# Attention and a gated projection on one core: nine full projection blocks per two batches, a second staging tile for V, and a re-dealt order

## The chip, the cores and the metric

The kernel runs on one core of a Trainium2 chip. Five instruction queues matter: PE (TensorE, matmuls and transposes), DVE (VectorE), ACT (ScalarE), POOL (GpSimd) and SP (SyncE), which here issues every DMA. Each queue is in order; they meet only at semaphores. The metric is the device time of one execution in microseconds, as a median over several runs.

## The reference

What is computed, with batch 8, 8 heads, 576 positions, head size 64 and model width 512:

```python
scores = scale * np.matmul(q, k.transpose(0, 1, 3, 2))
cum = np.cumsum(np.maximum(s, 0.0), axis=-1)
bias = -(cum[:, :, :, None] - cum[:, :, None, :])
scores = np.where(causal, -1e9, scores + np.minimum(bias, 0.0))
attn = softmax(scores)
x = (attn @ v), heads side by side            # (8, 576, 512)
gate = sigmoid(causal 5-tap convolution of x along the sequence, per channel)
out = (gate * (x @ w_val)) @ w_out
```

## The kernel before

Work is cut into 32 units n = 4b + p: batch b (8 of them) and pair of heads p (4 per batch). For each unit:

- q and k are cast to bf16 (L518; eight small casts for batch 0, two large ones for each later batch), transposed on PE (L557, unit by unit; the last 64 rows of q and k, the "tail", for a whole batch at once in L546) and copied from PSUM to the tile QKT (L561 and L549).
- Scores are computed key by key into pairs of PSUM banks (L566), in three steps of 1024 columns (512 for each of two heads), and each step goes through one exp on ACT (L592), 96 in all. The last 64 x 64 corner of every pair goes through a smaller exp (L578). POOL zeroes the future on the diagonal blocks (the mask, L598; L603 for the corners).
- The decay from s is folded into V: POOL or DVE multiplies the staging tile vst (f32) by w into Vp (bf16) with a column of ones (L528). The attention product (L613) is 30 matmuls per unit. DVE takes the reciprocal of the sums (L618) and normalizes into xn (L623).
- x is transposed (L631) and copied to xT (L635). Four taps of the convolution follow, each one DVE instruction (L647, L649) or two POOL ones (L644, L645); then a tanh on ACT (L653).
- Per batch: the value projection in eight groups of four matmuls (val, L660), each followed by glu on DVE (L666), which multiplies by the gate. Then the output projection.

The output projection before (L669 to L680) works batch by batch. 576 positions are five blocks; the fifth has 64 positions of its own. It is computed as a full block of 128 columns beginning at 448, and only its upper 64 rows are copied to an ot tile and stored: 40 blocks in all, each of four matmuls of 512 columns, a copy on ACT or DVE (L677) and a store (L680). Three ot tiles take turns.

One staging tile vst holds V of one batch; the loads for batch b wait for the four products of batch b - 1 that read it (L716).

What sets the order is a planner in the kernel (class Plan). Every task carries an engine, an assumed duration, a due time, the tasks it depends on and what it takes (PSUM banks, work tiles). The planner walks through time: each engine that is free takes the ready task with the smallest due time, and the resulting order is written out as the program. Due times are the unit's number plus an offset from the table DUE (with extra terms for the first two and the last two batches); where a task may run on several engines, a string of digits in CHOICE names the engine for each instance. On the chip, engines follow that order and wait for semaphores only; the planner's durations play no part there.

Places to look at: the head (L687 to L700: batch 0's loads in small pieces), the later batches' loads and casts (L702 to L720), the loops over units (L733 to L773), val and glu (L775 to L784), the projection (L785 to L792), and a check of all reciprocals near the end (L799 to L812), whose result the program reads before it finishes.

Of the kernel before, what the change touches and what calls it, by code (L numbers as in the profile page):

```python
# [10 lines left out]
FP32 = mybir.dt.float32  # L11
BF16 = mybir.dt.bfloat16
# [6 lines left out]
B, H, S, D = 8, 8, 576, 64  # L19
DM = 512  # L20
# [185 lines left out]
def pcol(kb, qb):  # L206
    if kb == qb:
        return kb * 128
    if qb == 4:
# [16 lines left out]
DUE = dict(w=-69.33, lwv=-4.26, lwo=-2.61, cwv=56.85, cwo=86.75, av=-11.07, norm=-74.98, xt=-16.64,  # L226
           xe=-86.49, tap=14.23, dtap=-1.47, tanh=-72.16, val=7.76, dval=0.88, out=11.28, dout=0.61,
           oute=87.55, qt=-4.79, qe=133.25, tt=-0.4, te=-149.08, s4=-20.03, vp=-7.1, cast=76.15, lqk=-1.56,
           mask=-123.76, lv=-49.38, av_e=7.71, av_l=6.68, cast_e=-31.51, cast_l=0.54, dout_e=-1.01,
           dout_l=-28.82, dtap_e=-7.57, dtap_l=16.17, dval_e=0.26, dval_l=0.84, lqk_e=-7.13, lqk_l=48.32,  # L230
           lv_e=98.37, lv_l=-92.01, mask_e=11.67, mask_l=11.41, norm_e=50.24, norm_l=38.99, out_e=0.39,
           out_l=42.92, oute_e=70.67, oute_l=-23.24, qe_e=-66.52, qe_l=-3.56, qt_e=4.39, qt_l=0.95,
           s4_e=8.96, s4_l=-14.16, tanh_e=58.9, tanh_l=56.45, tap_e=3.56, tap_l=-27.97, te_e=47.36,
           te_l=62.72, tt_e=19.75, tt_l=0.79, val_e=-3.44, val_l=-1.96, vp_e=-68.8, vp_l=29.32, xe_e=13.94,
           xe_l=0.22, xt_e=-5.82, xt_l=-13.61)


def due_of(b, name):
# [5 lines left out]
STAY = (0.1, 54.75)  # L244

CHOICE = dict(vp0="0100",
              cast="12200210",
              wts="00",
              te="10001100",
              qe="10100010000000001000100000100010",  # L250
              xe="00100010001000010000000000010010",
              tap="00000000100000000000001000000000000000010000100000000000000010000000000000001000001000001000100000000010000010010010001101110000",
              oute="1000001110101000010100010100011010000010")


class Plan:
# [22 lines left out]
    def run(self):  # L279
# [33 lines left out]
        while len(self.order) < len(self.tasks):  # L313
            started, later = False, []
            for e in engs:
# [36 lines left out]
                if e == "SP":  # L352
                    idle_at[e] = now + 0.06
                    dma_free = max(dma_free, now + 1.2) + us
                    t["done"] = dma_free + 0.8
                else:
                    idle_at[e] = t["done"] = now + us
# [21 lines left out]
def main_path(ctx, tc, q, k, v, s, moe_w_val, moe_conv_w, moe_w_out, out, okcnt):  # L379
# [9 lines left out]
    plan = Plan(dict(P=3, gp=2, th=6, ot=3, qkf=3))  # L389
# [484 lines left out]
```

## Time and profile before

| | us |
|---|---|
| median of 6 runs | 209.55 (209.17 to 211.56) |
| the profiled execution | 209.78 |
| its span | 208.1 |
| first exp of 1024 columns starts | 8.99 |
| last exp ends | 178.7 |
| last attention product ends | 180.7 |
| last copy of an output block ends | 202.4 |

A page's group line reads: source line, engine, operation, written tile <- read tiles, shape, count | total busy us, mean ns of one | idle time of the engine just before, and what ended most of it. Busy times of neighbours can overlap, so the busy time of an engine is less than the sum of its rows. In a view of busy time by stage, each row gives the stage, its length, busy us and number of instructions for each engine, then the granted TensorE clock, the share of time that the 16 DMA engines were busy, and their rate. In a timeline a row is start, length, engine, line, operation, and in brackets how long the engine was idle before and who released it.

The TensorE clock was granted in full for nearly all of the span (0.986 on average). DMA engines were busy without a pause up to about 110 us, since loads run ahead as far as buffers allow, and little used after that. Loads of V are made of runs of 256 bytes; 47,109 of 69,230 packets are under 512 bytes.

### The profile page before, as it was taken

How to read it: one execution, taken by the hardware profiler on the slowest of the kernel's cores; microseconds unless marked ns; L12 is line 12 of the kernel's file. 1: busy time of each engine (PE TensorE's matmuls, PEld its weight loads, DVE VectorE, ACT ScalarE, POOL GpSimd, SP SyncE). 2: the span in 40 equal slices, each digit the busy share in tenths (PEclk: the TensorE clock that was granted, in tenths of full speed). 3: DMA queues.
4: the chain of work that ended last, by engine and by line, in shares of the span. 5: the costliest groups of instructions: out<-in, count | busy, mean ns of one | idle time of the engine just before them, and what ended most of it. 6: DMA issues, size and time to landing. Idle time of an engine off the chain costs nothing.

```text
span 208.1 us, 6007 instructions
## 1 busy us (share of the span) xinstructions
PE 172.4 (83%) x2392; PEld 117.6 (57%) x2411; DVE 177.3 (85%) x311; ACT 163.3 (78%) x205; POOL 161.3 (78%) x179
## 2 busy tenths in 40 slices
PE   1688765899969997789899799989899999979950
PEld 0446553485737765467675657565576555755620
DVE  3847969989889998579999999999999998999710
ACT  3379897788999999987996997899987998553430
POOL 4265595599959998999499999958975898999300
PEclk9999998899999999999999999999999999999997
DMA  4999999999999898999999911941159120222551
GB/s 136 251 268 305 363 158 227 356 253 247 227 284 306 214 288 228 318 336 207 270 373 248 200 58 28 200 132 54 50 126 226 60 79 0 104 101 79 177 185 58
DMA packets 69230, 40.48 MB, mean 195 GB/s; under 512 B 47109, under 2 KB 63493, under 8 KB 69194
## 3 DMA queue, kind: packets, MB, share of 16 engines
q1 hardware_dynamic: 69194, 40.01, 72.1%
q8 instruction: 21, 0.34, 0.7%
q14 instruction: 15, 0.12, 0.2%
HBM read 30.57 MB, written 9.44 MB: 192 GB/s over the span
## 4 chain that ended last, share of the span: by engine, by line
DVE 25%; PE 21%; ACT 21%; issue 8%; DMA 8%; SPq 7%; POOL 7%; ACTq 0%; DVEq 0%
ACT P L592 12%; DVE gp L647 10%; PE banks L660 7%; DMA qkf<-in_moe_w_val_dram 6%; PE banks L672 6%; PE banks L613 4%; ACT QKT L561 3%; DVE xn L623 3%; DVE glu L666 3%; SPq L515 3%; DVE gp L649 3%; ACT th L653 3%; POOL Vp L528 2%; SPq L534 2%; PE banks L566 2%
## 5 line engine op out<-in xcount | busy, mean ns | idle before, releaser
L592 ACT ACTIVATE P<-banks 128x1024 bf16<-128x1024 f32 x96 | 94.9, 1038 | 11.4 <-PE banks L566 9.5
L647 DVE SCALAR_TENSOR_TENSOR gp<-banks,ratio,gp 128x574 f32<-128x574 bf16 (+2 forms) x85 | 67.5, 804 | 2.7 <-POOL gp L645 1.9
L598 POOL TENSOR_SCALAR_AFFINE_SELECT P<-P 128x512 bf16<-128x512 bf16 x64 | 39.4, 638 | 11.7 <-ACT P L592 11.5
L566 PE MATMUL banks<-QKT 64*128 64x128 bf16 (+4 forms) x576 | 38.4, 248 | 9.0 <-ACT P L592 5.3
L660 PE MATMUL banks<-xT,wv 128*128 128x288 bf16 x256 | 41.2, 291 | 2.2 <-DVE glu L666 0.9
L672 PE MATMUL banks<-wo,glu 128*128 128x512 bf16 x141 | 38.2, 379 | 2.6 <-ACT QKT L561 0.8
L528 POOL TENSOR_TENSOR Vp<-vst,w 128x650 bf16<-128x650 f32 x29 | 37.6, 1315 | 1.5 <-DMA vst<-in_v_dram 1.5
L613 PE MATMUL banks<-Vp,P 128*128 128x65 bf16 x960 | 35.7, 195 | 1.3 <-ACT P L592 1.2
L613 PEld LDWEIGHTS <-P 128*128 128x128 bf16 x960 | 33.8, 99 | 5.0 <-issue 2.1
L566 PEld LDWEIGHTS <-QKT 64*128 64x128 bf16 x576 | 20.0, 97 | 26.7 <-issue 20.4
L653 ACT ACTIVATE th<-gp,halfw 128x576 f32<-128x576 f32 x32 | 25.2, 792 | 7.1 <-DVE gp L647 3.6
L660 PEld LDWEIGHTS <-wv 128*128 128x128 bf16 x256 | 22.7, 98 | 13.6 <-issue 5.9
L666 DVE SCALAR_TENSOR_TENSOR glu<-th,banks 128x288 bf16<-128x288 f32 x64 | 27.8, 443 | 0.5 <-PE banks L660 0.3
L561 ACT COPY QKT<-banks 128x1024 bf16<-128x1024 bf16 x25 | 25.4, 1045 | 2.2 <-PE banks L557 2.1
L623 DVE TENSOR_TENSOR xn<-banks,recs 128x640 bf16<-128x640 f32 x32 | 26.2, 818 | 0.3
L677 ACT COPY ot<-banks 128x512 f32<-128x512 f32 (+1 forms) x26 | 15.2, 587 | 11.1 <-PE banks L672 6.9
L672 PEld LDWEIGHTS <-glu 128*128 128x128 bf16 x160 | 14.6, 97 | 15.5 <-issue 2.7
L649 DVE SCALAR_TENSOR_TENSOR gp<-xT,ratio,banks 128x576 f32<-128x576 bf16 x25 | 20.1, 808 | 1.6 <-ACT xT L635 0.9
L644 POOL TENSOR_TENSOR tmp<-xT,ratio 128x576 f32<-128x576 bf16 (+3 forms) x18 | 20.6, 1142 | 0.6 <-DVE xT L635 0.2
L645 POOL TENSOR_TENSOR gp<-tmp,gp 128x573 f32<-128x573 f32 (+2 forms) x11 | 15.7, 1429 | 3.1 <-DVE gp L647 2.3
L631 PE MATMUL banks<-ident,xn 128*128 128x128 bf16 x160 | 14.1, 219 | 3.0 <-DVE xn L623 1.1
L557 PE MATMUL banks<-ident,qb 128*128 128x128 bf16 x128 | 13.1, 227 | 2.1 <-ACT qb L518 1.3
(63 smaller groups left out, 168.0 us busy)
## 6 DMA issues: line engine op xcount, KB each, us to landing
out_dram<-ot SPq DMA_DIRECT2D x32, 256.0 KB, 2.8
qkf<-in_q_dram SPq DMA_DIRECT2D x7, 1024.0 KB, 8.8
qkf<-in_k_dram SPq DMA_DIRECT2D x7, 1024.0 KB, 8.4
vst<-in_v_dram SPq DMA_DIRECT2D x28, 256.0 KB, 5.1
vst<-in_v_dram SPq DMA_DIRECT2D x15, 128.0 KB, 4.2
first<-in_q_dram SPq DMA_DIRECT2D x4, 256.0 KB, 3.3
first<-in_k_dram SPq DMA_DIRECT2D x4, 256.0 KB, 3.5
tail<-in_q_dram SPq DMA_DIRECT2D x8, 128.0 KB, 8.1
```

The lines of the kernel that those rows point to most:

```text
L528: eng.tensor_tensor(Vps[b % 2][:, :, h], vst[:, :, h], w[:, :, b * 8 + 2 * p:b * 8 + 2 * p + 2].unsqueeze(3).to_broadcast([128, NKB, 2, 65 ...
L561: copy[e](QKTs[b % 2][:, :, p, 0:512].rearrange("d w (x j) -> d w x j", j=4), slot["qt", b, p].rearrange("d w (j x) -> d w x j", j=4))
L566: nc.tensor.matmul(ps[:, hh, c0:c0 + nq], QKTs[b % 2][r, 1, p, k0:k0 + 128], QKTs[b % 2][r, 0, p, q0:q0 + nq], **kw)
L592: nc.scalar.activation(out=slot["Pt", n][:, :, step * 512:(step + 1) * 512], in_=slot["s", n, step], func=AF.Exp, scale=0.125)
L598: nc.gpsimd.affine_select(out=d, in_=d, pattern=[[0, 4], [1, 128]], compare_op=ALU.is_ge, fill=0.0, base=0, channel_multiplier=-1)
L613: nc.tensor.matmul(ps[:, hh, qb * 65:qb * 65 + 65], lhsT, Vps[b % 2][:, kb, 2 * p + hh, :], start=(kb == 0), stop=(kb == qb))
L623: nc.vector.tensor_tensor(xns[b % 2][:, :, p * 128:(p + 1) * 128].rearrange("t g (h d) -> t h g d", h=2), pv[:, :, :, 0:64], recs[:, n].un ...
L647: nc.vector.scalar_tensor_tensor(gp[:, o:S], slot["x", n][:, 0:S - o], r, gp[:, o:S], ALU.mult, ALU.add)
L653: nc.scalar.activation(out=th, in_=slot["g", n], func=AF.Tanh, scale=halfw[:, n % 4, :])
L660: nc.tensor.matmul(ps, wv[:, dc, c * 128:(c + 1) * 128], xTs[b % 2][:, dc, 2 + o:290 + o], start=(dc == 0), stop=(dc == 3))
L666: nc.vector.scalar_tensor_tensor(glus[b % 2][:, c, o], slot["t", n][:, o], 1.0, slot["v", n, hf], ALU.add, ALU.mult)
L672: nc.tensor.matmul(ps, glus[b % 2][:, c, WIN[i]:WIN[i] + 128], wo[:, c, :], start=(c == 0), stop=(c == 3))
```

## The change

- **Projection.** Two batches share one glu tile of 1152 positions, so two batches are nine full blocks. An even batch issues four; the odd batch issues five, the first of which spans the boundary. There are 36 blocks instead of 40, all of 128 rows, all stored whole. glu waits for those old blocks only that read the half it overwrites.
- **Last batch.** Each block's projection is four tasks, one per chunk of 128 channels, each due on its own.
- **V.** Two staging tiles. Batch 1's V is loaded pair by pair, in 12 DMAs instead of 5, into the second tile; later batches wait for the products of two batches before. The second tile also serves as the landing place of five of batch 0's small q and k loads, so that its frame (ones and zeros) is set after their casts.
- **ot** has five tiles instead of three.
- **Engines.** Batch 0's tail cast and batch 1's two casts may run on DVE, ACT or POOL.
- **Planner.** A limit on how far SP may run ahead of the transfers (BEHIND), slightly different assumed durations, and new tables DUE, STAY and CHOICE.

The tables set the order and the engines anew. Counted over the built program: first casts DVE 3 to 1, ACT 2 to 5, POOL 3 to 2; tail copies (te) ACT 5 to 8, DVE 3 to 0; QKT copies (qe) 25 on ACT and 7 on DVE in both; xT copies DVE 26 to 18, ACT 6 to 14; taps DVE 110 to 108, POOL 18 to 20; ot copies ACT 26 to 29, DVE 14 to 7. Both of batch 1's casts are given to POOL ("22").

```diff
-STAY = (0.1, 54.75)
-
-CHOICE = dict(vp0="0100",
-              cast="12200210",
+STAY = (1.42, 130.04)
+
+BEHIND = 9.7
+
+CHOICE = dict(cast1="22",
+              tailc="2",
+              vp0="0100",
+              cast="11121201",
...
                 if e == "SP":
-                    idle_at[e] = now + 0.06
                     dma_free = max(dma_free, now + 1.2) + us
+                    idle_at[e] = max(now + 0.06, dma_free - BEHIND)
...
-    plan = Plan(dict(P=3, gp=2, th=6, ot=3, qkf=3))
+    plan = Plan(dict(P=3, gp=2, th=6, ot=5, qkf=3))
...
+    vraw = [one.tile([128, NKB * 8 * 65], FP32, name=f"vst{j}") for j in range(2)]
+    vsts = [a.rearrange("p (i h d) -> p i h d", i=NKB, h=8) for a in vraw]
+
+    def v_frame(j):
+        nc.gpsimd.memset(vsts[j][:, :, :, 64:65], 1.0)
+        nc.gpsimd.memset(vsts[j][0:64, 4, :, :], 0.0)
...
-    glus = two("glu", [128, 4, S], BF16)
+    glu2 = one.tile([128, 4, 2 * S], BF16, name="glu")
+    glus = [glu2[:, :, 0:S], glu2[:, :, S:]]
+    outf = out.rearrange("b s d -> (b s) d")
...
-    def outp(b, i):
-        ps = slot["o", b, i] = bank(("o", b, i), 128, DM)
-        for c in range(4):
-            nc.tensor.matmul(ps, glus[b % 2][:, c, WIN[i]:WIN[i] + 128], wo[:, c, :], start=(c == 0), stop=(c == 3))
+    def outp(b, i, cs):
+        if cs[0] == 0:
+            slot["o", b, i] = bank(("o", b, i), 128, DM)
+        o = (4 * (b % 2) + i) * 128
+        for c in cs:
+            nc.tensor.matmul(slot["o", b, i], glu2[:, c, o:o + 128], wo[:, c, :], start=(c == 0), stop=(c == 3))
...
     def store(b, i):
-        nc.sync.dma_start(out=out[b, kbo[i]:kbo[i] + kbs[i], :], in_=slot["ot", b, i][128 - kbs[i]:128, :])
+        r = b // 2 * 2 * S + (4 * (b % 2) + i) * 128
+        nc.sync.dma_start(out=outf[r:r + 128, :], in_=slot["ot", b, i])
...
+            if b == 1:
+                t = add("POOL", 0.7, DUE["vf"], lambda: v_frame(1), [T["cast", 0, i % 2, i // 2] for i in range(5)])
+                ts = [[add("SP", 1.45, DUE["lv1"] + DUE["lv1d"] * p, lambda p=p: load_v_pair(1, p), [t])] for p in range(4)]
+            else:
+                ts = [[add("SP", 1.45, n0 + due("lv") + i * 0.01, lambda b=b, i=i: load_v_block(b, i),
+                           [T["vp", b - 2, p] for p in range(4)]) for i in range(NKB)]] * 4
...
-        for i in range(NKB):
-            hfs = [(0,), (0,), (0, 1), (1,), (1,)][i]
-            t = T["out", b, i] = add("PE", 0.88, n0 + due("out") + due("dout") * i, lambda b=b, i=i: outp(b, i),
-                                     [T["glu", n0 + c, hf] for c in range(4) for hf in hfs] + [t_wo],
-                                     take=[("bank", ("o", b, i))])
+        for i in range(4 + b % 2):
+            own = [(0,), (0,), (0, 1), (1,), (1,)][i]
+            need = lambda c: [T["glu", n0 + c, hf] for hf in own] + ([T["glu", n0 - 4 + c, 1]] if b % 2 and i == 0 else [])
+            if b == B - 1:
+                t = None
+                for c in range(4):
+                    t = add("PE", 0.22, n0 + DUE["ol"] + DUE["old"] * i + DUE["doc"] * c, lambda b=b, i=i, c=c: outp(b, i, (c,)),
+                            need(c) + [t_wo, t or T["xt", n0 + 3], T["val", n0 + 2, 1]], take=[] if c else [("bank", ("o", b, i))])
+                T["out", b, i] = t
+            else:
+                t = T["out", b, i] = add("PE", 0.88, n0 + due("out") + due("dout") * i, lambda b=b, i=i: outp(b, i, range(4)),
+                                         [d for c in range(4) for d in need(c)] + [t_wo], take=[("bank", ("o", b, i))])
```

## The prediction

> **What bounds the kernel now.** I read the page's busy times first, then the busy time of each engine by stage, then the rows by form, then the instructions of the last 30 us in order.
>
> ```profile
> PE 172.4 (83%) x2392; PEld 117.6 (57%) x2411; DVE 177.3 (85%) x311; ACT 163.3 (78%) x205; POOL 161.3 (78%) x179
> ```
>
> Four engines lie within 16 us of each other, so no single one explains 208.1 us. The stages say more. I cut where batch 0's last exp ends (27.2), where the masks of pair 7, batch 1's last, end (50.5), at 101, and where the last exp (178.7) and the last copy (202.4) end.
>
> ```profile
> core 0: us, PE busy (x) PEld busy (x) DVE busy (x) ACT busy (x) POOL busy (x), PEclk, DMA share, GB/s
> 0.00:27.20 27.20, 16.65 (x226) 11.84 (x226) 18.62 (x34) 17.68 (x24) 14.58 (x31) 1.00 0.94 261
> 27.20:50.50 23.30, 19.39 (x282) 13.60 (x283) 20.83 (x36) 18.56 (x23) 18.78 (x21) 0.93 1.02 244
> 50.50:101.00 50.50, 44.15 (x687) 31.68 (x691) 43.95 (x75) 47.50 (x59) 47.05 (x48) 1.00 1.03 269
> 101.00:178.70 77.70, 71.67 (x1052) 48.45 (x1060) 75.47 (x136) 70.06 (x87) 65.92 (x70) 1.00 0.52 134
> 178.70:202.40 23.70, 20.58 (x155) 12.03 (x154) 18.41 (x34) 9.47 (x16) 14.95 (x12) 1.00 0.40 140
> ```
>
> The reader is to see that DVE is 97% busy (75.47 of 77.70) from 101 us on: it bounds the second half. In the middle, from 27.2 to 178.7 (151.5 us), DVE is busy for 140.3, ACT 136.1, PE 135.2, POOL 131.7. The end is another regime: exps are done, and the deferred projections drain through DVE and PE.
>
> ```profile
> 175.90 2.83 ACT L592 ACTIVATE P<-banks 128x1024 bf16<-128x1024 f32 x3
> ...
> 196.05 4.48 PE L672 MATMUL banks<-wo,glu 128*128 128x512 bf16 x19
> ...
> 199.81 0.58 ACT L677 COPY ot<-banks 128x512 f32<-128x512 f32 x1 [1.25 <-DMA out_dram<-ot]
> 201.82 0.58 ACT L677 COPY ot<-banks 128x512 f32<-128x512 f32 x1 [1.43 <-DMA out_dram<-ot]
> ```
>
> Five blocks of the last projection run in one row, and two copies wait for a store to free one of three ot tiles.
>
> **The change part by part.** Rows that price it:
>
> ```profile
> L672 PE MATMUL banks<-wo,glu 128*128 128x512 bf16 x141 | 38.2, 379 | 2.6 <-ACT QKT L561 0.8 <-DVE gp L647 0.3 <-issue 0.2
> L635 DVE COPY xT<-banks 128x576 bf16<-128x576 bf16 x26 | 11.6, 450 | 2.4 <-PE banks L631 2.3
> L635 ACT COPY xT<-banks 128x576 bf16<-128x576 bf16 x6 | 4.0, 661 | 0.2 <-DVE ok L802 0.2
> L677 ACT COPY ot<-banks 128x512 f32<-128x512 f32 x20 | 11.8, 589 | 9.7 <-PE banks L672 6.6 <-DMA out_dram<-ot 2.7 <-ACT P L592 0.3
> L677 DVE COPY ot<-banks 128x512 f32<-128x512 f32 x12 | 8.2, 684 | 2.2 <-PE banks L672 2.1
> ```
>
> *Projection blocks, 40 to 36.* 16 matmuls and 4 copies go. A lone matmul's 379 ns is latency; in a row they cost 4.48/19 = 0.236 us, so PE loses 16 x 0.24 = 3.8. A 64-row copy costs what a full one does (580 against 589 ns on ACT), so the four copies go at full price. Three of the four blocks leave the stretch after the last attention product: 13 blocks stand there before, 10 after.
>
> *The new choices of engine.* They outweigh the blocks. Copies of ot: ACT 26 to 29, DVE 14 to 7. Copies of xT: ACT 6 to 14, DVE 26 to 18. Tail transposes (te): ACT 5 to 8, DVE 3 to 0. First casts: ACT 2 to 5, DVE 3 to 1, POOL 3 to 2; the first tail cast goes from DVE to POOL. Taps: POOL 18 to 20, DVE 110 to 108. ACT: 3 x 0.589 + 8 x 0.661 + 3 x 0.595 + 3 x 0.618 = +10.7. DVE: 7 x 0.684 + 8 x 0.45 + 3 x 0.417 + 2 x 0.80 + 2 x 0.55 + 0.41 = -12.8. All rows of ACT add to 176.5 against 163.3 busy, those of DVE to 195 against 177.3, because neighbours overlap; scaled so, ACT +9.9 and DVE -11.6. POOL: 2 taps of 1.14 + 1.42, 0.7 for the second frame of V, 0.6 tail cast, less a 0.6 cast: +5.8.
>
> *A rule against the row.* The Trainium skill (Perfetto Trace Analysis, Identifying the Most-Contended Engine) takes the engine of highest occupancy as the one to relieve first. Occupancy names DVE, so by the rule its 11.6 us are worth up to 11.6: 198. The stage rows refuse that: ACT stands 4.2 us behind DVE in the middle and receives nearly all that DVE gives up. I follow the rows.
>
> *The middle, summed.* By the order of instructions of the changed kernel, 3.3 of ACT's 9.9 come before batch 0's last exp, and behind the last exp nothing is added (one ot copy fewer, one xT copy more): 136.1 + 6.6 = 142.7. DVE sheds 4.0 in batch 0 and 0.3 at the end: 140.3 - 7.3 = 133.0. On POOL 16 taps stand ahead of the last mask instead of 12, so 146.3 to 157.0 there; about 1.4 of it is in batch 0: middle 131.7 + 9.3 = 141.0. PE stays near 135. ACT is the new bound, POOL close behind. How dense can a bound engine be? The busiest engine of each middle stage has 20.83 + 47.50 + 75.47 = 143.8 of 151.5, 94.9%; the last stage alone 97.1%. At 97.1% the middle takes 147.0 (-4.5), at DVE's own 92.6% 154.1 (+2.6). I take 95.7%: the first stage's 89.4% I move halfway to full, since V of batch 1, now requested at 26.3 behind the last read of V of batch 0, gets its own tile. 142.7/0.957 = 149.1: **-2.4**.
>
> *Two tiles of V, and the queues.* POOL waits 1.5 us in all for V's loads, so the tile is worth 0 to 2 us, counted in that density. Below zero: V of batch 1 becomes 12 issues in place of 5; SP sends them past the tails of batch 2, w_out and q, k of batch 2, with DMA at 1.02 in that stage. Seven more issues at 0.5 us are 3.5 us of SP time, hidden while those loads are already waiting for engines; w_out is needed at 46.8. If that cover fails, up to 3.5 us of delay reach batch 2's casts on POOL. On POOL four Vp products (4 x 1.3 = 5.2) now stand ahead of batch 1's first mask; ACT runs on into three P tiles meanwhile.
>
> *Head.* SP now sends conv_w and both tails (0.55 + 0.7 + 0.7) before q, and s later. q was cast 2.8 us after issue (2.01 to 4.82), so ACT's first cast moves from 4.82 to about 5.6; tail copy 0.6, cast of k 0.6, transposes 0.8, copy of QKT 1.0 (it was on DVE), a cast and the small exp follow on ACT: first exp at 10.4 against 8.99. Then ACT has fewer gaps (about 7 us in batch 0 against 9.5): 21.0 + 7.0 = 28.0, **+0.8**.
>
> *End.* DVE is 14.96 of 15.2 busy from the last attention product (180.7) to the last five blocks (195.9). The new order has 14.1 us of rows there against 16.2, so -2.1 if DVE stays the limit and 0 if the chain tap, tanh, glu does; PE (2.9 less) and POOL (5.1 less) give room. I take -1.0. With five ot tiles the last copy follows its matmul (200.5) by 0.2 + 0.6 instead of ending at 202.4: -1.1. Together **-2.1**, ends -1.1 and -3.2. The last store's 5.7 us remain.
>
> *Chunk by chunk, and the casts of batch 1.* In the built order the last 20 projection matmuls still run block by block, four chunks each, behind all eight val groups. The edit is worth nothing as placed; had it worked, only 5 of 20 would follow the last glu and 15 x 0.236 = 3.5 us would go. Both casts of batch 1 stay on POOL: zero. glu now waits for fewer old projection blocks; all its waits were 0.5 us: zero. The other edits are due times, whose effect is the order used above.
>
> Sum: 0.8 - 2.4 - 2.1 = -3.7. Against the profiled span that is 204.4; that execution took 209.78, 0.23 above the median of 209.55, so the median should be **205.9**.
>
> **The rivals.** *POOL becomes the bound (slower).* Its work behind mask 7 is 157.0 - 36.6 = 120.4 us against 112.9. Never idle, it ends its last mask at 50.5 + 120.4 = 170.9; before, it idled 15.3 us in that stretch, 11.5 us over the whole run waiting for exps. My forecast leaves it 6; equality with before comes at about 9 (0.8 lost at the head, 2.1 regained at the end), slower by 1% at about 11, and its old 15.3 gives 209.55 + 7.5 - 2.1 = 215. For it: masks, casts, Vp and taps stand in one queue, and the taps now come earlier. Against: POOL waits mostly when it is ahead, and with more work it is ahead less. *It comes to nothing.* At 94% density the middle takes 151.8, and with the head and -1.1 at the end it is 209.55. For it: the four engines' total in the middle rises from 543.3 to 551.7; 94.9% was the measured density. *Much faster.* ACT at 97.1% (-4.5), the head at 0 and the end at -3.2: 201.9. For it: DVE held 97% for 78 us. Against: three engines would be above 91% at once.
>
> **How the numbers follow.** Forecast (203 to 207.4): 0.42. Much faster (below 203): 0.14. Nothing: 0.25. POOL: 0.19, of which a half lies under 213. About 1%, 2.1 us, can be told from no change: faster 0.56, same 0.25, slower 0.19. The range, 201.8 to 211.2, leaves out a few per cent below and over a tenth above; 203 to 207.4 is the forecast's own.
>
> **What would show it.** DVE near 166 busy, ACT near 173, POOL near 167, PE near 168.6; first exp near 10.4; last exp near 177; no ot copy waiting for a store; the last 20 projection matmuls still in a row of about 4.5 us. I am wrong if the last exp ends past 180 with POOL or ACT full of gaps, or if the end, counted from the last exp, is not shorter than 29.4.

## The result, and the profile after

The changed kernel takes 211.5 us as a median (209.87 to 214.64) against 210.1 (208.12 to 213.45) for the kernel before on the same chips: the ratio is 1.0069, with a 95% interval from 1.0048 to 1.0091. It is slower by 0.7%, where 1.7% faster was forecast (205.9 against 209.55); 211.5 also lies above the upper end of the range. The profiled execution of the changed kernel took 210.05 us, 1.4 below its own median, so the trace accounts for 0.3 us of the difference and not for the rest.

The trace is enough to see which terms of the sum came out otherwise:

| | before | after | forecast | measured |
|---|---|---|---|---|
| head: start to batch 0's last exp | 27.2 | 28.9 | +0.8 | +1.7 |
| middle: to the last exp | 151.5 | 154.7 | -2.4 | +3.2 |
| end: from the last exp to the span's end | 29.4 | 24.7 | -2.1 | -4.7 |
| span | 208.1 | 208.3 | -3.7 | +0.2 |

The page's line of busy times, and the stages that the prediction cut, in the changed kernel (columns as before: stage, length, busy us of PE, its weight loads, DVE, ACT and POOL, granted clock, DMA share, GB/s):

```profile
PE 172.0 (83%) x2378; PEld 118.1 (57%) x2395; DVE 168.4 (81%) x288; ACT 170.7 (82%) x222; POOL 167.6 (80%) x185
```

```profile
27.20:50.50 23.30, 19.46 (x275) 14.09 (x274) 17.30 (x26) 19.64 (x24) 21.11 (x22) 0.78 0.98 245
50.50:101.00 50.50, 44.44 (x641) 30.84 (x645) 42.56 (x73) 42.36 (x56) 46.46 (x45) 0.93 1.03 261
101.00:178.70 77.70, 71.67 (x1090) 49.21 (x1096) 73.37 (x128) 76.42 (x99) 72.50 (x78) 1.00 0.53 141
178.70:202.40 23.70, 22.07 (x199) 13.58 (x199) 21.05 (x40) 13.08 (x20) 12.58 (x11) 1.00 0.36 134
```

The work moved as forecast (DVE to ACT and POOL), and from 101 us on ACT is the bound as forecast: 76.42 of 77.70, 98%. The stage from 50.5 to 101 is where it fails: ACT did 47.50 us of work there before and does 42.36 now, although it was given more to do. A cut at 87.0, about where batch 2's last normalization now ends (87.2; 79.5 before), shows it more sharply. First before, then after:

```profile
50.50:87.00 36.50, 31.20 (x461) 21.89 (x464) 32.09 (x52) 35.62 (x45) 33.13 (x35) 1.00 1.04 272
87.00:178.70 91.70, 84.62 (x1278) 58.24 (x1287) 87.33 (x159) 81.95 (x101) 79.84 (x84) 1.00 0.59 154
```

```profile
50.50:87.00 36.50, 32.11 (x431) 21.31 (x434) 29.58 (x51) 28.44 (x38) 32.80 (x32) 0.91 1.03 253
87.00:178.70 91.70, 84.00 (x1298) 58.73 (x1307) 86.35 (x150) 90.34 (x116) 86.16 (x91) 1.00 0.61 163
```

ACT works 28.44 of 36.5 us instead of 35.62. After 87 us it hardly stands still (90.34 of 91.7), and batches 4 to 7 take 75.0 us where they took 81.3 (from the end of batch 3's last normalization to that of batch 7's). Batches 2 and 3 take 53.4 where they took 45.2. What ACT and PE wait for there stands in their timelines of the changed kernel (start, length, engine, line, operation, and in brackets the idle time before and who ended it):

```profile
63.04 0.78 ACT L670 ACTIVATE th<-gp,halfw 128x576 f32<-128x576 f32 x1 [1.08 <-POOL gp L662]
...
74.80 0.78 ACT L670 ACTIVATE th<-gp,halfw 128x576 f32<-128x576 f32 x1 [3.44 <-POOL gp L662]
```

```profile
64.78 1.10 PE L583 MATMUL banks<-QKT 64*128 64x64 bf16 x8 [2.09 <-ACT P L609]
```

A tanh waits for a tap on POOL, the exps stand behind the tanh, and the scores wait for the exps. POOL's own queue, in the changed kernel:

```profile
53.90 1.89 POOL L534 CAST kb<-qkf 128x2048 bf16<-128x2048 f32 x1
...
58.53 1.89 POOL L534 CAST qb<-qkf 128x2048 bf16<-128x2048 f32 x1 [2.19 <-DVE gp L664]
60.39 1.14 POOL L661 TENSOR_TENSOR tmp<-xT,ratio 128x572 f32<-128x572 bf16 x1
61.61 1.40 POOL L662 TENSOR_TENSOR gp<-tmp,gp 128x572 f32<-128x572 f32 x1
```

Batch 2's cast of k starts at 53.90 (50.50 before), batch 3's cast of q at 58.53 (56.04 before), and the tap that the tanh at 63.04 waits for stands right behind it. The bracket of the cast of q names DVE, but by the trace its transfer landed only at 58.48. The load of that q is issued by SP later than before, behind loads of V that the second tile lets through. Before, then after:

```profile
46.14 1.61 SPq L515 DMA_DIRECT2D qkf<-in_q_dram  x1
47.80 5.21 SPq L540 DMA_DIRECT2D vst<-in_v_dram  x3
```

```profile
46.81 1.40 SPq L557 DMA_DIRECT2D vst<-in_v_dram  x1
48.30 3.20 SPq L531 DMA_DIRECT2D qkf<-in_q_dram  x1
```

At the end, no copy of an output block waits for a store any more; ACT's last copy follows its matmuls (ACT's timeline of the changed kernel):

```profile
201.89 0.58 ACT L696 COPY ot<-banks 128x512 f32<-128x512 f32 x1 [1.14 <-PE banks L692]
```

### The profile page after: what moved, and what is told of

The parts are those of the page before. It is cut to its first block, busy times and chain, and to the rows that moved or that the text cites. A ratio compares the mean times of both kernels' runs of the same rounds, so it can differ in the third digit from the quotient of the medians.

```text
span 208.3 us, 5968 instructions
## 1 busy us (share of the span) xinstructions
PE 172.0 (83%) x2378; PEld 118.1 (57%) x2395; DVE 168.4 (81%) x288; ACT 170.7 (82%) x222; POOL 167.6 (80%) x185
## 4 chain that ended last, share of the span: by engine, by line
DVE 28%; ACT 28%; PE 23%; issue 10%; POOL 6%; DMA 2%; SPq 1%; DVEq 0%; ACTq 0%; POOLq 0%
ACT P L609 16%; DVE gp L664 10%; PE banks L630 7%; PE banks L677 7%; DVE xn L640 5%; DVE glu L683 4%; ACT QKT L578 4%; PE banks L583 4%; DVE gp L666 4%; PE banks L692 3%; POOL gp L662 3%; POOL tmp L661 2%; ACT th L670 2%; DMA vst<-in_q_dram 2%; ACT ot L696 2%
## 5 line engine op out<-in xcount | busy, mean ns | idle before, releaser
L664 DVE SCALAR_TENSOR_TENSOR gp<-banks,ratio,gp 128x574 f32<-128x574 bf16 (+2 forms) x82 | 65.9, 810 | 3.2 <-POOL gp L662 2.1
L583 PE MATMUL banks<-QKT 64*128 64x128 bf16 (+4 forms) x576 | 40.0, 255 | 13.9 <-ACT P L609 8.6
L630 PEld LDWEIGHTS <-P 128*128 128x128 bf16 x960 | 35.0, 101 | 6.9 <-issue 4.1
L583 PEld LDWEIGHTS <-QKT 64*128 64x128 bf16 x576 | 19.4, 98 | 29.4 <-issue 21.7
L692 PE MATMUL banks<-wo,glu 128*128 128x512 bf16 x127 | 33.6, 379 | 1.3 <-issue 0.2
L677 PEld LDWEIGHTS <-wv 128*128 128x128 bf16 x256 | 23.8, 100 | 12.4 <-issue 4.4
L683 DVE SCALAR_TENSOR_TENSOR glu<-th,banks 128x288 bf16<-128x288 f32 x64 | 27.2, 446 | 3.7 <-PE banks L677 3.5
L661 POOL TENSOR_TENSOR tmp<-xT,ratio 128x572 f32<-128x572 bf16 (+3 forms) x20 | 23.0, 1148 | 1.3 <-DVE xT L652 0.8
L696 ACT COPY ot<-banks 128x512 f32<-128x512 f32 x29 | 17.2, 607 | 7.3 <-PE banks L692 6.3
L662 POOL TENSOR_TENSOR gp<-tmp,gp 128x572 f32<-128x572 f32 (+2 forms) x14 | 19.8, 1417 | 1.6 <-DVE gp L664 0.5
L692 PEld LDWEIGHTS <-glu 128*128 128x128 bf16 x144 | 12.9, 98 | 14.2 <-issue 1.8
L534 POOL CAST qb<-qkf 128x2048 bf16<-128x2048 f32 x7 | 13.2, 1890 | 2.7 <-DVE gp L664 2.2
```

The lines of the kernel that those rows point to most:

```text
L583: nc.tensor.matmul(ps[:, hh, c0:c0 + nq], QKTs[b % 2][r, 1, p, k0:k0 + 128], QKTs[b % 2][r, 0, p, q0:q0 + nq], **kw)
L630: nc.tensor.matmul(ps[:, hh, qb * 65:qb * 65 + 65], lhsT, Vps[b % 2][:, kb, 2 * p + hh, :], start=(kb == 0), stop=(kb == qb))
L664: nc.vector.scalar_tensor_tensor(gp[:, o:S], slot["x", n][:, 0:S - o], r, gp[:, o:S], ALU.mult, ALU.add)
L677: nc.tensor.matmul(ps, wv[:, dc, c * 128:(c + 1) * 128], xTs[b % 2][:, dc, 2 + o:290 + o], start=(dc == 0), stop=(dc == 3))
L683: nc.vector.scalar_tensor_tensor(glus[b % 2][:, c, o], slot["t", n][:, o], 1.0, slot["v", n, hf], ALU.add, ALU.mult)
L692: nc.tensor.matmul(slot["o", b, i], glu2[:, c, o:o + 128], wo[:, c, :], start=(c == 0), stop=(c == 3))
```

## The experiments

Each ratio is to the kernel before, run on the same chip, with its 95% interval.

**The code apart from its order.** The change is two things: other code (36 blocks, two V tiles, five ot tiles, chunks) and another order. To hold an order fixed, the planner was made to take tasks only in a given sequence for each engine, from a table AT of places; the engines came from CHOICE as before:

```diff
+        queue = {e: sorted((t for t in self.tasks if t["eng"] == e), key=lambda t: (t["key"], t["n"])) for e in engs}
...
+                    if t is not queue[e][0]:
+                        continue
...
+    for t in plan.tasks:
+        t["key"] = AT[name_of(t)]
```

e5_old_order: the changed code with the places and engines that the kernel before had.

> The changed code (nine full output blocks per two batches, the last batch's projection chunk by chunk, two V tiles, five ot tiles), but every engine's queue in the order of the kernel before, and every copy and tap on the engine that it had before; only the first block of batch 5's projection moves up, ahead of the gate work that overwrites its rows. Theory (the order of the queues costs, not the code): the code alone takes four output blocks away, whose four ot copies were all ACT's (about 0.62 us each, 2.5 us), and ACT was busy 89 to 91% of the middle before; so 207.5 to 209.5, faster than before by 0.3 to 1.2%, the last norm of batch 2 near 79 and of batch 3 near 101 in the profile. Rival (the code itself costs, as by the V loads in pairs, the wait of a block for two batches, or five stores behind each other): 211 to 213, as slow as the changed kernel, with batch 2 ending near 83 or later.

209.0 us, 0.9954 (0.9929 to 0.9979). The code alone is faster by about 0.5%. Between this and the changed kernel (1.0069) lies 1.15%, 2.4 us, and only the order and the engines differ. So the order is what made it slower. In e5's trace batch 2 ends at 81.9 and batch 3 at 103.1 (79 and 101 expected, 87.2 and 111.2 in the changed kernel), and the last copy ends 0.6 us after the last projection matmul (202.65 + 0.59 against 198.13 + 4.48), where the kernel before needed 1.9.

```profile
198.13 4.48 PE L687 MATMUL banks<-wo,glu 128*128 128x512 bf16 x20
```

```profile
202.65 0.59 ACT L691 COPY ot<-banks 128x512 f32<-128x512 f32 x1 [0.28 <-PE banks L687]
```

e8_old_ot3 and e4_ot3 take two ot tiles away again, from e5 and from the changed kernel:

```diff
-        ot = slot["ot", b, i] = work("ot", (b, i), [128, DM], FP32)
+        ot = slot["ot", b, i] = one.tile([128, DM], FP32, name=f"ot{len(used) % 3}")
+        used.append(i)
```

> The changed code in the old order, as in e5, with three ot tiles in turn instead of five, the order of the queues kept. Theory (of what the code gains, the end's ot wait is the larger part): the last copies wait for stores again as before, so 0.8 to 1.3 us more than e5: about 210, level with the kernel before (ratio to before 0.999 to 1.002). Rival (the gain is the four blocks that went, the fourth and fifth tile are idle in this order): within 0.4 us of e5, ratio about 0.995.

> The changed kernel with its order kept, but only three ot tiles in turn, as before. If the wait of the last copies for a store was worth what the prediction took for it, the end is 1.1 us later and the run about 212. If the end is set by TensorE's row of matmuls alone, no change (within 0.4).

e8 took 210.75, 1.0043 (1.0017 to 1.0070): 0.9% over e5, about 1.9 us, which is more than all that e5 won. In its trace the last copy ends 2.9 us behind the last matmul (0.6 in e5), and no copy waits for a store ahead of the last row of projection matmuls: in this order the end accounts for the whole loss. e4 took 222.87, 1.0575 (1.0517 to 1.0634), some 11 us over the changed kernel where 1.1 had been expected. The new order asks for the fourth and fifth tile all along, not only at the end; by the row of its ACT copies they stood waiting for stores for 7.2 us:

```profile
L699 ACT COPY ot<-banks 128x512 f32<-128x512 f32 x29 | 17.1, 602 | 16.7 <-DMA out_dram<-ot 7.2 <-PE banks L693 5.2 <-PEq L889 3.3
```

**One suspect at a time.** The first suspects were the loads and the taps. e1_loads lets SP send k of batches 2 and 3 ahead of V of batch 2 and of later tails, e2_taps gives five taps (units 4, 6 and 8) from POOL to DVE, e3_both does both:

```diff
+    behind(k2, V2[0], V2[1])
...
+    for n, sh in ((4, 1), (4, 4), (6, 4), (8, 2), (8, 3)):
+        to(T["tap", n, sh], "DVE")
```

> The changed kernel with its order kept, except that SP sends k of batch 2 directly behind q of batch 2, k of batch 3 ahead of the tails of batch 4, and the loads of V of batch 2 behind them. Theory LOADS (the second tile lets V and tails go ahead of q and k while the DMA engines are full, so batches 2 and 3 start late): the first exp of batch 2 comes at 55 to 56 instead of 59.0, batch 2 (normalized at 87.2) ends 2 to 4 us earlier, the run is 2 to 3.5 us shorter than the changed kernel, about 208. Theory TAPS (POOL's taps in batches 1 and 2 hold up casts and tanh): within 0.7 us of the changed kernel.

> The changed kernel with its order kept, except that five taps (units 4, 4, 6, 8, 8) run on DVE, at the same place, instead of POOL. POOL loses 5 x 2.55 = 12.8 us of work between 47 and 77, DVE, which idles there, gains 4. Theory TAPS: ACT's waits for POOL's taps (1.1 and 3.4 us) go, the casts of batches 2 and 3 come up to 2.5 us earlier, batch 2's pitch falls from 29.4 to 25 or less, the run is 3 to 5 us shorter, about 207. Theory LOADS: at most 1 us. Theory CLOCK (the half-speed stretches of TensorE, from 26.8, 40.5 and 64.7 on, are a cause and not only a consequence): the stretch from 64.7 goes together with the wait of PE at 62.7, and the gain is larger than the tanh waits alone, 4.5.

> Both edits of the two runs before. If loads and taps are separate causes the gains add: 5 to 8 us under the changed kernel, about 204. If they are one chain (a late cast holds the tap behind it) the gain is that of the larger one alone.

e1: 210.9, 0.9998 (0.9960 to 1.0036); e2: 212.8, 1.0101 (1.0058 to 1.0144); e3: 213.5, 1.0111 (1.0028 to 1.0194). The loads may give 0.7% back, at the edge of what the intervals tell. In e1 the q of batch 3 goes ahead of three of V's five loads and lands at 57.5 instead of 58.5; its cast starts at 58.47 all the same, behind a tap and the cast of k. The taps give nothing, and e2's trace shows where the time goes: the tanh at 63.81 no longer waits, but PE then runs 16 matmuls of val in 4.00 us at half clock. The attention product stands behind them, its normalization and a tap on DVE behind that, and the tanh at 76.94 waits for this tap:

```profile
63.81 0.82 ACT L671 ACTIVATE th<-gp,halfw 128x576 f32<-128x576 f32 x1
...
76.94 0.78 ACT L671 ACTIVATE th<-gp,halfw 128x576 f32<-128x576 f32 x1 [4.35 <-DVE gp L665]
```

```profile
70.01 4.00 PE L678 MATMUL banks<-xT,wv 128*128 128x288 bf16 x16 [0.58 <-DVE gp L665]
```

e6_tanh puts the tanh of unit 4 behind two exps; e7_val also puts val and glu of units 4 and 5 behind the attention products of units 8 and 9. e14_wo_cast puts DVE's cast of w_out, which waits 2.06 us for its load, behind three taps and two glus; e15_wo_tail also moves the transposes of batch 2's tail later. In AT, e14 against the changed kernel's order, and e15's addition:

```diff
-('slot', 'wo'): 37.91
+('slot', 'wo'): 42.5
...
-('tails', 2): 39.75, ('tail_T', 2): 40.65, ('tail_evac', 2): 41.6
+('tails', 2): 41.6, ('tail_T', 2): 43.9, ('tail_evac', 2): 44.7
```

> The changed kernel with one instruction moved: on ACT the tanh of unit 4, which at 61.9 us waited 1.08 us for a POOL tap with three exps of batch 2 behind it, stands behind two of those exps. Theory (clock): the exps come 1 us earlier, the PE gap of 2.09 us before 64.78 shrinks to about 1, PE keeps its full clock, the value products of units 4 and 5 at 68.6 take about 2.1 us instead of 3.57, and batch 2 ends 2 to 3 us earlier (84 to 85 instead of 87.2); a part of it reaches the end: 208.5 to 210.5. Rival (the gap is only a sign of an engine that has nothing to do yet; the clock falls anyway, or what follows waits for the POOL tap of unit 6): within 0.3% of the changed kernel, 211 to 212, batch 2's end within 1 us of 87.2.

> The run before, and in addition the value products and glus of units 4 and 5 behind the attention products and norms of units 8 and 9 on PE and DVE. Theory (the order on PE holds batch 2): the products of units 8 and 9, which stood behind 16 value products at half clock until 71.95, start 3 us earlier, batch 2 ends 3 to 4 us earlier than 87.2 and the whole is 1 to 3 us faster than the changed kernel: 208 to 210. Rival (work is only exchanged: the glus, and the banks that they give back, come as much later as the norms come earlier): 210.5 to 213, with batch 3 ending near 111 or later whatever batch 2 does.

> The changed kernel with one instruction moved: on DVE the cast of w_out, which at 39.8 us waits 2.06 us for its load and then takes 1.69 us, stands behind the three taps and two glus of batch 0 that followed it. Theory (two instructions that stand waiting at the head of a queue, this one and the transposes of batch 2's tail on PE, are what the stretch from 30 to 50 us costs): 0.5 to 1 us less than the changed kernel, ratio to before 1.001 to 1.004. Rival (the cost is spread over the order of the whole stretch; the taps that follow wait for the POOL tap that ends at 42.4 anyway): ratio 1.004 to 1.011.

> The run before, and in addition batch 2's tail out of the way of batch 1: its cast on POOL behind the masks of unit 5, its transposes on PE, which at 43.4 us waited 0.67 us ahead of unit 6's scores and unit 4's attention products, behind these, its copy on ACT behind two exps of unit 6. Theory: 1.5 to 2.5 us less than the changed kernel, ratio to before 0.995 to 1.000, and the half clock of 40 to 47 us gone or shorter. Rival: ratio 1.004 to 1.011, batch 1 ending within 1 us of 57.8.

e6: 212.0, 1.0108 (1.0063 to 1.0153); e7: 211.0, 1.0056 (1.0028 to 1.0085); e14: 211.5, 1.0063 (1.0038 to 1.0087); e15: 211.1, 1.0049 (1.0023 to 1.0075). All four miss: none can be told from the changed kernel. Batch 2 ended at 88.2 and 87.5 in e6 and e7 (87.2 in the changed kernel). None of the waits that were moved carries the loss by itself.

**Which stretch of the order.** e9_old_start takes batches 0 and 1 and the weights in the old order, and batches 2 to 7 in the new one. e10_new_order is a third order: e5's up to 30 us, then places and engines shifted over all batches. (In e9 an engine may take a task up to 1 us of place ahead of the head of its queue.)

> The changed code; the work of batches 0 and 1 (their loads, casts, attention, gate and projection, and the load of the weights) in the order and on the engines of the kernel before, the work of batches 2 to 7 in the changed kernel's order, on its engines. Theory A (the order of batches 2 and 3 costs, the late start is made up by slack): batch 1 ends at 56 to 57 in the profile, batches 2 and 3 still take about 53 us together, and the time is that of the changed kernel within 0.5%: ratio to before 1.003 to 1.011. Theory B (the start, 1.6 us late in the changed kernel, is most of what the order costs): 1.6 to 2.4 us less than the changed kernel, ratio to before 0.995 to 1.000, batch 3 ending at 108 to 109 instead of 111.2.

> The changed code in a third order: that of e5 as far as about 30 us; from there the places in the queues and the engines of copies and taps are shifted one by one so that fewer engines wait, over all batches. Theory (the order decides, and neither of the two is the best for this code): 202 to 206, 2 to 4% faster than before, batch 2 ending near 79, batch 3 near 100, last exp near 177 and no half clock longer than before's 5 us. Rival (what orders exchange is waits at one place for waits at another; the engines' sums of 160 to 178 us leave no more): 208 to 211.

e9: 209.1, 0.9957 (0.9931 to 0.9984); e10: 209.6, 0.9948 (0.9919 to 0.9976), not the 202 to 206 of one theory. So the new order of the last six batches, their loads included, costs nothing once the first two batches and the weights are worked in the old one; what costs lies in how those are worked. e9 has the time that theory B expected, but not its signs: batch 3 ends at 110.1 (108 to 109 expected), and batches 2 and 3 still take 52.0 us, as theory A had it for a slow kernel. The next four split by time: every task whose place in the old order is below a cut keeps that place and its engine; the rest takes the new one, and what the new order has before the cut goes right behind it. In effect:

```diff
-        t["key"] = new[name]
+        t["key"] = old[name] if old[name] < CUT else max(new[name], CUT)
```

with CUT at 12, 30, 40 and 50 us of the old order.

> The changed code; every queue in the order and on the engines of the kernel before for the instructions that stood in about its first 12 us (the loads of s, batch 0 and batch 1, the first casts, transposes and scores), then in the changed kernel's order. Theory (the head is what the start costs): batch 0 ends at 32.2 to 32.7 instead of 33.8 and that is kept, so 1.5 to 2.5 us less than the changed kernel: ratio to before 0.995 to 1.001. Rival (it is not the head, but the order of batch 0's gate and batch 1's attention from 12 to 50 us): as the changed kernel, ratio 1.003 to 1.010.

> As the run before, but with the old order as far as about 30 us. Theory of the head: nothing over the run before. Rival: part of what e9 gained, ratio between the run before and the run behind this; the loads of batch 2's q and k are in it, so if those count, most of the gain appears here.

> As e11 to e13, with the old order as far as about 40 us. In the old order unit 2's taps, tanh and value products and unit 4's attention products stand before 40 us, in the new one behind it, where the loads of batch 2's V and of batch 3's q come first; what the old order has before 50 us beyond that is unit 6's attention, its norm, unit 4's taps on DVE and the cast of batch 2's k. If the stretch from 30 to 40 us decides: ratio to before 0.989 to 0.997, as e13. If that from 40 to 50 us decides: 1.005 to 1.012, as e12. If both do: between, 0.998 to 1.004.

> As the two runs before, with the old order as far as about 50 us, the changed kernel's order behind it. Theory (what is late at 50 us, above all batch 0's projection, of which nothing was done in the changed kernel and 7.4 products in the kernel before, is paid in batch 2): at least the gain of e9, ratio to before 0.990 to 0.997, batch 2 ending at 82 to 84 and no half clock between 60 and 75. Rival (the head alone decides): the same as e11 within 0.4%.

| old order up to | us | ratio |
|---|---|---|
| nothing (the changed kernel) | 211.5 | 1.0069 (1.0048 to 1.0091) |
| 12 us (e11) | 211.25 | 1.0103 (1.0051 to 1.0156) |
| 30 us (e12) | 211.95 | 1.0110 (1.0073 to 1.0147) |
| 40 us (e18) | 212.32 | 1.0094 (1.0066 to 1.0122) |
| 50 us (e13) | 208.10 | 0.9894 (0.9847 to 0.9941) |
| all (e5) | 209.01 | 0.9954 (0.9929 to 0.9979) |

Nothing is won up to 40, and 4.2 us between 40 and 50. e11 did bring the first exp back from 10.94 to 9.19, and lost it again: its batch 1 ended at 60.3, later than the changed kernel's 57.8. e13 beats both kernels, the one before by about 1.1%. The signs expected of it did not come: batch 2 ended at 85.8 (82 to 84 expected), and the clock was at half from 64.5 to 71.3 us (none from 60 to 75 expected).

In the traces of all runs with the new order behind 50 us, e4 apart, the span ends 96.8 to 97.5 us after batch 3's last normalization (107.0 before, 106.0 in e5). What these runs win or lose against each other therefore lies ahead of it.

e18 and e13 differ only in the ten us between the cuts. Stages of each, e18 first:

```profile
40.00:50.00 10.00, 8.04 (x126) 5.30 (x121) 7.45 (x15) 8.09 (x9) 9.79 (x10) 1.00 1.13 301
50.00:60.00 10.00, 8.46 (x148) 5.99 (x145) 9.46 (x15) 6.51 (x10) 3.99 (x4) 1.00 1.04 235
60.00:76.00 16.00, 8.13 (x108) 5.32 (x106) 6.79 (x12) 8.32 (x10) 14.99 (x16) 0.68 1.10 304
```

```profile
40.00:50.00 10.00, 9.60 (x160) 6.80 (x158) 9.12 (x18) 8.80 (x11) 8.01 (x9) 0.97 1.08 301
50.00:60.00 10.00, 8.11 (x109) 5.16 (x106) 9.86 (x16) 7.55 (x11) 7.32 (x8) 1.00 1.07 231
60.00:76.00 16.00, 13.55 (x187) 9.28 (x184) 11.59 (x21) 10.62 (x14) 13.31 (x14) 0.79 1.11 303
```

In e18 POOL stands still for 6 of the 10 us after 50 and is then full while ACT, DVE and PE are half idle. Its queues say what it waited for (SP, POOL and ACT in e18):

```profile
48.40 4.05 SPq L552 DMA_DIRECT2D vst<-in_v_dram  x3
52.55 0.82 SPq L526 DMA_DIRECT2D qkf<-in_q_dram  x1
```

```profile
60.86 1.89 POOL L529 CAST qb<-qkf 128x2048 bf16<-128x2048 f32 x1 [6.79 <-DMA qkf<-in_q_dram]
62.71 1.14 POOL L656 TENSOR_TENSOR tmp<-xT,ratio 128x572 f32<-128x572 bf16 x1
63.93 1.39 POOL L657 TENSOR_TENSOR gp<-tmp,gp 128x572 f32<-128x572 f32 x1
```

```profile
65.35 0.77 ACT L665 ACTIVATE th<-gp,halfw 128x576 f32<-128x576 f32 x1 [6.17 <-POOL gp L657]
```

The q of batch 3 is sent at 52.55, behind V of batch 2, and cast at 60.86; a tap of batch 1 stands behind that cast, a tanh behind the tap, the exps behind the tanh. Part of this is the splice's own: it holds three loads of V back to 48.40, right ahead of q, where the changed kernel had sent two of them at 36.23. In e13 SP sends q first and V behind it, and the taps of unit 4 are on DVE:

```profile
49.68 1.61 SPq L526 DMA_DIRECT2D qkf<-in_q_dram  x1
51.34 7.53 SPq L552 DMA_DIRECT2D vst<-in_v_dram  x5
```

```profile
56.78 1.90 POOL L529 CAST qb<-qkf 128x2048 bf16<-128x2048 f32 x1 [1.64 <-DMA qkf<-in_q_dram]
```

*What does not make the difference.* The chain of late load, late cast and late tap is what the traces of the changed kernel and of e18 show, but it is not by itself the cost. In the changed kernel and in e1 to e4, e6, e7, e11, e12 and e14 to e18 the cast of q starts between 57.8 and 61.3 us, in e5 and e13 at 56.5 and 56.8; but e9 sends V and then this q as the changed kernel does, casts it as late, and is as fast as e5:

```profile
48.67 3.32 SPq L526 DMA_DIRECT2D qkf<-in_q_dram  x1
```

```profile
59.12 1.89 POOL L529 CAST qb<-qkf 128x2048 bf16<-128x2048 f32 x1 [1.08 <-DMA qkf<-in_q_dram]
```

In e2 and e3 no tap stands behind that cast on POOL, in e3 the cast starts at 57.79, and both are slow. Nor is it how little ACT does: from 27.2 to 87 us ACT does even less in e9 and e13 than in the changed kernel (first the changed kernel, then e9, then e13):

```profile
27.20:87.00 59.80, 51.57 (x704) 35.41 (x708) 46.88 (x76) 48.08 (x62) 53.91 (x53) 0.86 1.01 250
27.20:87.00 59.80, 49.15 (x688) 34.87 (x687) 51.28 (x83) 46.84 (x59) 45.96 (x46) 0.93 0.98 234
27.20:87.00 59.80, 51.61 (x683) 35.89 (x684) 49.38 (x80) 46.33 (x61) 48.46 (x49) 0.86 1.00 245
```

*What is left.* Taken together, e9 and e13 against e18 leave the tasks of batches 0 and 1 that the old order has between 40 and 50 us: above all the attention products of units 5 and 6, the taps of unit 4 on DVE, its tanh, and a block of batch 0's projection, which the new order places 3 to 10 us later. One mark separates every trace: batch 1's second tanh on ACT starts at 56.1 to 59.3 us in the kernel before, e5, e8 (whose loss is that of its ot tiles), e9, e10 and e13, where unit 4's tanh stands ahead of unit 5's, and at 63.0 us or later in the changed kernel and all the other runs, where it stands behind (e1, which lies between in time, 64.2). This is a mark and not a shown cause: no run moved batch 1's gate or attention forward by itself (e6 and e7 move parts of them back), nor was the chunk by chunk projection tried alone. How the 4.2 us divide among these tasks is open.

**The TensorE clock.** The changed kernel's clock is lower (0.95 on average over its runs, 0.976 before). Over the runs of the kernel before, 0.01 of clock goes with 0.83 us, so the clock was a rival cause worth 2 us. e16_warm2 keeps the changed kernel's order and places 18 unread matmuls into PE's waits between 23 and 45 us; e17_warm3 places 27:

```diff
+    def dummies(j):
+        ps = bank(("warm", j), 128, DM)
+        for _ in range(2):
+            nc.tensor.matmul(ps, ident, warm, start=True, stop=True)
```

> The changed kernel, its order kept, with 18 products added that nobody reads (128x512, two at each of nine places between 23 and 45 us where PE stood waiting ahead of scores, of a tail's transposes or of an attention product; into a free bank, from a tile of ones). Theory (the waits themselves cost little, the half clock that follows them does: over the runs of the kernel before, 0.01 of mean clock go with 0.83 us, and the changed kernel's clock is 0.027 lower): the half clock at 26 to 31 and at 40 to 47 us goes or shrinks, the mean clock rises from 0.95 to 0.965 or more, and the time falls by 1 to 2 us: ratio to before 0.997 to 1.002. Rival (the clock falls where there is nothing to do, and the time is set by what PE waits for): the clock rises, but the ratio stays at 1.004 to 1.012, the upper end if the added products, 4 us of PE at full clock, stand in the way.

> As the run before, with three products at each of the nine places instead of two (27, 6 us of PE at full clock). Theory: a clock at least as high, and the same time or less. Rival: slower than the run before by the 0.5 to 2 us of PE that are added.

The clock rose to 0.965 and 0.969, and the time did not fall: 212.3, 1.0109 (1.0063 to 1.0155), and 212.6, 1.0116 (1.0076 to 1.0157). In e16 the half clock between 40 and 48 us is gone; first the changed kernel, then e16:

```profile
40.00:48.00 8.00, 6.79 (x77) 3.91 (x71) 4.58 (x6) 7.30 (x10) 6.33 (x8) 0.57 1.11 309
62.00:74.00 12.00, 8.99 (x121) 5.89 (x121) 7.63 (x13) 8.31 (x10) 11.92 (x14) 0.72 1.11 325
```

```profile
40.00:48.00 8.00, 5.59 (x56) 2.69 (x54) 5.03 (x8) 7.75 (x9) 7.42 (x10) 1.00 1.10 309
62.00:74.00 12.00, 7.39 (x67) 4.19 (x65) 7.73 (x12) 9.85 (x13) 11.92 (x14) 0.72 1.10 320
```

ACT was busy for 7.30 of 8 us there with the half clock, and for 7.75 with the full one; the stall from 62 to 74 stays. Other runs say the same: at a mean clock of 0.965 stand e13 (0.9894), e9 (0.964; 0.9957) and e16 (1.0109), so the mean clock does not set the time. The low clock looks more like a sign of PE's waits than their cause. What the added matmuls cost in themselves was not measured apart, so a small gain could be hidden under them.

## Why the prediction was wrong

*The step that failed* is the middle: "At 97.1% the middle takes 147.0 (-4.5), at DVE's own 92.6% 154.1 (+2.6). I take 95.7%". From batch 0's last exp to the last exp, the changed kernel took 154.7 us instead of the forecast 149.1, and ACT was busy for 140.5 of them:

```profile
28.88:183.55 154.67, 138.88 (x2047) 96.20 (x2059) 136.75 (x231) 140.46 (x181) 142.02 (x144) 0.95 0.75 193
```

The work was sized about right (ACT 142.7 forecast, POOL 141.0 forecast and 142.0 measured); the density was not: 90.8% of the middle for ACT, where 95.7% was assumed. The 94.9% from which the prediction started is put together from the busiest engine of each stage: DVE, then ACT, then DVE. Reckoned in this way the changed kernel's stages have 95.0% (POOL 21.11, POOL 46.46 and ACT 76.42 of 151.5 us), as much as before. But no single engine had that density over the whole middle, and the prediction divided the work of one engine, ACT, by it. ACT is the bound only from 101 us on; ahead of that POOL was busier. With DVE's own 92.6% the working gives 154.1, close to what was measured; that figure stood in it and was passed over. From 27.2 to 87 us ACT had 80.4% (19.64 + 28.44 of 59.8), where it had been 90.6%.

The allowance for the second tile pointed the wrong way: "worth 0 to 2 us, counted in that density" moved the density up, and in that first stage ACT then had 84.3%. The prediction named what would break it, "up to 3.5 us of delay reach batch 2's casts on POOL", and set that at zero. Batch 2's cast of k came 3.4 us later, the next q 2.5 us later; but the cast of k had its data at 52.4 and stood behind a tap until 53.9, and e9 shows that such a delay need not cost.

How the thin middle turns into time is a second question. In e9 and e13 the middle, cut in the same way, is 155.7 and 155.5 us, longer still, and both are faster than the kernel before: the new order of the later batches gives the time back at the end. That the order is what costs is shown by e5 (1.15%), that it is the order of batches 0 and 1 and the weights by e9, and that it is the stretch of 40 to 50 us by e13 against e18; which task in it, is open.

*Head, +0.8 forecast, +1.7 measured.* Right in kind: first exp at 10.94 (10.4 forecast). But e11 shows that this term does not add up with the others: with the first exp back at 9.19 the kernel was no faster.

*End, -2.1 forecast, -4.7 measured.* The term for the ot tiles was right for the trace's end: -1.1 forecast, -1.2 in e5 (1.87 to 0.63 us from last matmul to last copy). In e8 against e5 the two extra tiles are worth 1.9 us, more than this term. The remaining gain at the end is not all a gain: the last exp came 4.9 us later, and so left less work behind it (DVE 16.4 us, 18.4 before). The last copy ends at 202.47, as before (202.4).

*Zeros.* Chunk by chunk: the last 19 projection matmuls of the trace (20 were forecast) still stand in a row of 4.54 us behind the last val, as forecast:

```profile
193.35 4.08 PE L677 MATMUL banks<-xT,wv 128*128 128x288 bf16 x32
197.27 4.54 PE L692 MATMUL banks<-wo,glu 128*128 128x512 bf16 x19
```

*The signs named beforehand.* DVE 168.4 (166 forecast), ACT 170.7 (173), POOL 167.6 (167), no copy waiting for a store: all as forecast, and all true of a kernel that is slower. Only PE's 172.0 (168.6) is off, at the lower clock. The last exp near 177 was missed: it ended at 183.6, past the 180 that had been named as the mark of a failure. As a mark it is weaker than it looks, since it ends at 182.5 in e9 and at 182.8 in e13, which are faster than the kernel before. The end, counted from the last exp, is shorter than 29.4 (24.7), so the other sign of being wrong did not come.

*The rivals.* "POOL becomes the bound" was right in number: it had equality with the kernel before at about 9 us of idle time on POOL behind mask 7, and 1% slower at about 11. POOL had 10.5 there (131.4 us, 120.9 of them busy; 120.4 forecast), and the kernel is 0.7% slower. Its mechanism is not borne out: e2 takes five taps off POOL in that stretch and is no faster (1.0101), so its number may be luck. "It comes to nothing" had the right thing in it, a density below the forecast's (94%), and a change of 0.7% is under the 1% that the prediction said can be told from none. The rule that was set against the rows (relieve DVE, 198) is further off than the rows (205.9): DVE did 8.9 us less work, and the time rose. The 0.5% between e5 and the kernel before is what the edits of code brought; the order took back more than twice that.

## What to carry to other kernels

When a change re-deals the order of in-order queues, the sum of work per engine tells where the bound goes, not how dense it will be. A density put together from the busiest engine of each stage is one that no engine has; divide an engine's work by its own. To find which part of an order costs, splice the old order and the new one, by time and by batch: here that narrowed the cost to ten microseconds of two batches, where most moves of single tasks had found nothing. And hold a chain of late events that one trace shows against kernels that lost nothing as well: here e9 had the same late load and the same late cast.

## What was not expected of the hardware

The granted clock fell to half after short waits of PE. In the changed kernel PE never waited longer than 0.88 us in the 6 us before the half clock of 40.8 to 47.6 us (its timeline there):

```profile
35.25 2.13 PE L677 MATMUL banks<-xT,wv 128*128 128x288 bf16 x16
...
38.27 0.62 PE L583 MATMUL banks<-QKT 64*128 64x64 bf16 x8 [0.46 <-DVE glu L683]
39.77 0.62 PE L583 MATMUL banks<-QKT 64*128 64x128 bf16 x12 [0.88 <-ACT P L609]
40.69 0.54 PE L583 MATMUL banks<-QKT 64*128 64x320 bf16 x4 [0.30 <-ACT P L609]
41.16 2.22 PE L677 MATMUL banks<-xT,wv 128*128 128x288 bf16 x8
```

A val matmul took 133 ns before (2.13 us for 16) and 278 ns behind it (2.22 for 8). The Trainium skill (TensorE: Matmul & The Clock Gate, "HAM oscillation") gives as its rule that PE-idle gaps above about 3.4 us are to be avoided; here several waits of under 1 us were followed by the half clock, and the measurement decides. That the kernel was no faster with this stretch at full clock (e16) was the second surprise.
